# Segment attention in two layer pairs: a new layout for stored keys and queries, one kept set of output weights, a split last value projection, and regrouped closing norms

## The chip, the cores and the metric

The kernel runs on one core of a Trainium2 chip. A core has several engines, each with its own queue of instructions that it works through in order: TensorE (PE in the profile) multiplies matrices and writes to PSUM, VectorE (DVE) and ScalarE (ACT) work element by element and move PSUM results to SBUF, GpSimd (POOL) does small copies here, and SyncE (SP) issues transfers. SP, ACT and POOL each issue DMA transfers, which 16 DMA engines carry out; main memory is called DRAM. Engines wait for each other by semaphores.

The metric is the time of one execution on the device in microseconds (us). The time before is the median of three runs.

## What is computed

Four residual layers follow each other, A, B, A, B, here numbered 0 to 3. The input is 2048 rows of 640 numbers.

```python
def _A_ref(x, mem0, Wq, Wk, Wv, Wo, seg_len):        # 32 heads of 192, seg_len 32, 8 memory rows
    mem = mem0
    for s in range(n_seg):                             # 64 segments, one after the other
        h = jnp.concatenate([mem, x[:, 32*s:32*s + 32, :]], axis=1)      # 40 rows
        q, k, v = (einsum('btd,dhe->bhte', h, W) for W in (Wq, Wk, Wv))
        p = softmax(where(mask, einsum('bhqe,bhke->bhqk', q, k) * scale, -1e9))
        o = einsum('bhte,hed->btd', einsum('bhqk,bhke->bhqe', p, v), Wo)
        mem = o[:, :M, :]                              # the next segment's memory rows
        outs.append(o[:, M:, :])
    return jnp.concatenate(outs, axis=1)

def _B_ref(x, wqkv, w_phi, wo):                        # linear attention, 32 heads of 20
    ...
    o = num / den
    return o.reshape(B, S, D) @ wo

x = x + _A_ref(_layernorm(x), ...)
x = x + _B_ref(_layernorm(x), ...)
x = x + _A_ref(_layernorm(x), ...)
x = x + _B_ref(_layernorm(x), ...)
```

A segment's memory rows are an output of the segment before it, so the 64 segments of a layer A form a chain: 8 output rows have to be complete before the next segment's first projection can start.

## The kernel before

**Layer A** (`layer_A`, L632) has three parts.

*Preparation* (`A_pre`, L718). Of the 32 input rows of a segment the last 8, its tail rows, don't take part in what the chain hands on, apart from their keys and values being seen by others. Their queries, keys and values are computed ahead for all segments in large matmuls. The work is cut into two halves `h` of 32 segments and four rounds `r` of 8 heads. Each (half, round) computes K and Q for 256 rows into a staging tile `st` (two of them take turns, `sts`, in the space `wo_mid` that later holds output weights) and stores it to DRAM in one transfer, `kqb_d` (L877, named kqb<-arena in the profile: a staging row holds 32 segments x 192 numbers for one of 128 partitions). This store goes through SP's queue in layer 0 and through ACT's in layer 2. V goes through two small tiles in `wo_end` to `vb_d` (L899, vb<-arena, 8 transfers on POOL's queue for each half and round). After the last rounds the output weights are loaded over the staging space (`early_wo`, `late_wo`, L702 to L707), so these loads wait for the stores to land.

*The chain* (`A_chain`, L905; the segment loop starts at L1108). The order of instructions is written by hand (`manual_schedule`). A segment runs its four rounds in the order 0, 1, 2, 3 when it is even and 3, 2, 1, 0 when it is odd; the last, 63, is odd. In each round PE projects Q and K (`q_or_k`) and V (`project`) from `hT`, the 32 chain rows of the segment: 8 memory rows and 24 input rows. Each projection has five steps `b` of four matmuls. The weights of rounds 1 and 2 stay in SBUF, as do those of the steps 0 and 1 of rounds 0 and 3; the steps 2 to 4 of rounds 0 and 3 share slots, which SP refills during a segment's first round for its last (`load_slot`, L665 and L670). The prepared tail keys and queries are read back with `load_kqb` (L946, L948 at the DMA; one transfer per segment and round on POOL's queue, two rounds ahead into two buffers) and copied beside the chain's own by POOL (`extra_kq`, L951 to L956); tail values come by `extra_v` (L960, Vp<-vb). Then `scores` (L1014, L1019), an exponential on ACT (`weigh`, L1072), column sums on PE (`sums`, L1086), a reciprocal by Ln and Exp on ACT and a multiply on DVE (`normalise`, L1091 to L1093), and `attend` (L1027) follow. A round's attention runs while the next round's projections do. The results of the 32 chain rows are multiplied by the round's output weights into `W` (`wo_round`, L1049, matmul at L1054, 12 steps of four matmuls); those of the 8 tail rows are kept and stored (`keep_tail`, `store_tail`, L1047, otb<-otb). The output weights of rounds 1 and 2 stay in `wo_mid`; those of rounds 0 and 3 share `wo_end`, so that `load_wo` (L682, loads at L687 and L689) fetches the set of the segment's last round when the set of its first has been used. `keep_busy` adds matmuls without use.

*The closing product* for the tail rows (`post_steps`, L1224, matmuls at L1243 and L1244): in groups of 16 segments, the stored tail results are fetched (`fetch_tails`, L1210), rearranged (`spread_tails`), and multiplied by all four sets of output weights. For this the last segment loads both sets, 0 and 3, one into `wo_end`, one into `low`, the space of the resident projection weights.

**Layer B** (`layer_B`, L248) ends in a loop over four groups `g` of 512 rows: `attention` computes six column chunks `c`, each with two products (L559) and a spread of the denominators (L562) on PE, a copy on ACT (L564) and a multiply on DVE (L565); `output_rows` multiplies by `wo` (L410), adds the residual for four row blocks of 128 and stores them. In layer 1 the layer norm for the next layer A is worked out on the way: `ln_moments` (L217, DVE), `ln_deviation` (L229, ACT), `ln_apply` (L237, DVE and ACT), then a store to `xnext_dram`. `finish_rows` (L572) does the last two for a row block of the group before, called inside the attention. Layer 3 has no such norm.

The DMA semaphores of a queue are used in turn: before an issue, the engine waits until the transfer that used that semaphore last has landed.

Of the kernel before, what the change touches and what calls it, by code (L numbers as in the profile page):

```python
# [8 lines left out]
P = 128  # L9
BF16 = mybir.dt.bfloat16  # L10
F32 = mybir.dt.float32
ACT = mybir.ActivationFunctionType
ALU = mybir.AluOpType
# [102 lines left out]
class Kernel:  # L116
# [131 lines left out]
    def layer_B(self, x_dram, at_dram, xout_dram, xnext_dram, li, bp, post):  # L248


        nc, tc, KC, D = self.nc, self.tc, self.KC, self.Dm
# [14 lines left out]
        wo = self.view(take(NC_ * D * 2), NC_ * D * 2).rearrange("p (c m) -> p c m", m=D)  # L266
# [24 lines left out]
        with tc.tile_pool(name=f"B{li}_kv", bufs=1, space=bass.MemoryType.PSUM, reuse_waits="tile") as kvp, \  # L291
# [260 lines left out]
            def attention(g, hl):  # L552
                tk = slice(512 * g, 512 * g + 512)
                oT = oTs.next().rearrange("p (c t) -> p c t", c=NC_)
                for c in range(NC_):
                    mc = sizes[c]
                    pn = bank("ps_num")
                    for sg in range(2):
                        nc.tensor.matmul(pn[0:mc, :], lhsT=kvm[0:mc, sg, c, 0:mc], rhs=phi[0:mc, sg, c, tk], start=(sg == 0),  # L559
                                         stop=(sg == 1))  # L560
                    pe = bank("ps_e")
                    nc.tensor.matmul(pe[0:mc, :], lhsT=expc[0:64, c, 0:mc], rhs=hl, start=True, stop=True)  # L562
                    rx = rxs.next()
                    nc.scalar.activation(out=rx[0:mc, :], in_=pe[0:mc, :], func=ACT.Copy)  # L564
                    nc.vector.tensor_tensor(out=oT[0:mc, c, :], in0=pn[0:mc, :], in1=rx[0:mc, :], op=ALU.mult)  # L565
                    if c > 0:
                        finish_rows()
                return oT

            unfinished = []  # L570

            def finish_rows():  # L572
                if unfinished:
                    ob, m, rows = unfinished.pop(0)
                    xn = xns.next()
                    self.ln_apply(bp, ob, m, self.ln_deviation(bp, m), xn, True)
                    nc.gpsimd.dma_start(out=xnext_dram[rows, :], in_=xn[:])

            def output_rows(g, oT):
                for b in range(4 * g, 4 * g + 4):  # L580
# [7 lines left out]
                    if xnext_dram is not None:  # L588
                        unfinished.append((ob, self.ln_moments(bp, ob, 6), rows))

            hl = [denominators(0, side_bank), denominators(1, bank)]
            for g in range(NG):
# [5 lines left out]
                output_rows(g, oT)  # L598
            while unfinished:
                finish_rows()  # L600
# [31 lines left out]
    def layer_A(self, xn_dram, at_dram, li, x_raw=None):  # L632
# [4 lines left out]
        PW = 1536  # L637
        self.kqb_d = dram.tile([NSEG, P, NR, 192], BF16, name=f"kqb{li}")
        self.vb_d = dram.tile([NSEG, NR, 2, 8, 896], BF16, name=f"vb{li}")
# [78 lines left out]
    def A_pre(self, xn_dram, li, load_matrix, piece, wo_mid, wo_end, lay_out_wo, early_wo, x_raw):  # L718
# [12 lines left out]
        with ExitStack() as es:  # L731
# [102 lines left out]
            for h, ri, r in steps:  # L834
# [41 lines left out]
                stq = nc.scalar if x_raw is None else nc.sync  # L876
                stq.dma_start(out=self.kqb_d[SH * h:SH * h + SH, :, r, :].rearrange("s p f -> p s f"), in_=st)  # L877
                if x_raw is not None:
# [26 lines left out]
    def A_chain(self, xn_dram, at_dram, li, load_slot, piece, load_wo, late_wo, wo_mid, wo_end, low):  # L905
# [3 lines left out]
        with tc.tile_pool(name=f"A{li}_ch", reuse_waits="tile", bufs=1) as sp, \  # L909
# [36 lines left out]
            def load_kqb(s, r):  # L946
                kqb = sp.tile([P, 192], BF16, name="kqb", tag="kqb", bufs=2)
                nc.gpsimd.dma_start(out=kqb[:], in_=self.kqb_d[s, :, r, :])  # L948
                return kqb
# [96 lines left out]
            def store_tail(otb, s, r):  # L1046
                nc.gpsimd.dma_start(out=self.otb_d[:, s, 96 * r:96 * r + 96], in_=otb[:, :, :].rearrange("p c t -> p (c t)"))  # L1047

            def wo_round(W, r, OT, first, last, part=range(12)):  # L1049
                w = wo_end[:, :] if r in (0, 3) else wo_mid[:, 7680 * (r - 1):7680 * r]  # L1050
                for i in part:
# [56 lines left out]
            for s in range(NSEG):  # L1108
                W = pop.tile([P, 512], F32, name="ps_w", tag="w")
                order = rounds(s)  # L1110
                L = NR - 1

                def q_or_k(m, n):
# [23 lines left out]
                v_rows(pv, 0)  # L1137
                Ep = None
                for n in range(L):
                    raw = q_or_k("Q", n + 1)  # L1140
# [13 lines left out]
                    if n == 1:  # L1154
                        wo_round(W, order[n - 1], OT, True, False)
                        if n == 1:
                            load_wo(order[L])
                            if s == NSEG - 1:
                                tails = [self.fetch_tails(0, low)]
                                load_wo(3, low[:, 0:7680])  # L1160
                                tails.append(self.fetch_tails(1, low))
                    if n + 1 < L:
# [4 lines left out]
                pv = v_banks()  # L1167
                project(hT, pv, "V", L, s, range(KC))
                v_rows(pv, L)
                OT1 = OT  # L1170
                wo_round(W, order[L - 2], OT1, False, False, range(4))
                S, E = weigh(True)
# [4 lines left out]
                store_tail(otb, s, order[L - 1])  # L1177
                wo_round(W, order[L - 2], OT1, False, False, range(4, 6))
                sums(S, E)
                wo_round(W, order[L - 2], OT1, False, False, range(6, 12))  # L1180
                normalise(S, E)
# [42 lines left out]
    def post_steps(self, ops):  # L1224

        nc = self.nc
        at_dram, wo_mid, wo_end, low = self.post_args
        wo = [wo_end[:, :], wo_mid[:, 0:7680], wo_mid[:, 7680:15360], low[:, 0:7680]]

# [58 lines left out]
```

## Time and profile before

| | |
|---|---|
| runs | 3598.71, 3606.52, 3606.56 us, median 3606.52 |
| profiled execution | 3619.27 us; span 3617.5 us; mean granted TensorE clock 0.992 |
| bytes moved by DMA | 933.32 MB in 517,905 packets, 141,066 of them under 512 B |
| L977, projections, ps_qk and ps_v on PE | 998.2 + 519.2 us busy |
| L1054, output weights on PE | 18,432 matmuls, 451.7 us busy |
| layer 0, chain of segments | from 168.4 us to about 1546 us |
| layer 2, chain of segments | from 1980.9 us to about 3364 us |

A row of the profile names line, engine, operation and tiles (written <- read), partitions x elements, and how often (x). In a timeline the first two numbers are the start and the duration in us, and the brackets hold the engine's idle time before and what ended it. In the list of DMA issues come the KB of one transfer and the median time from issue to landing. The queues q1 and q10 are those that SP and ACT issue to, q0 is POOL's. The granted clock is the share of TensorE's full clock that its throttle let through; where it is below 1, matmuls take longer.

### The profile page before, as it was taken

The page shows a single profiled execution, that of the slowest core. Times are in us where ns is not written, and L with a number is a line of the kernel's source. Part 1 is how long each engine was busy: PE and PEld are TensorE (multiplying, and loading weights), DVE is VectorE, ACT ScalarE, POOL GpSimd, SP SyncE. Part 2 cuts the span into 40 slices and gives each one's busy share as a digit, 9 for nine tenths or more (in the row PEclk, how much of TensorE's full clock was granted, in tenths as well). Part 3 has the DMA queues.
Part 4 walks back from the last instruction along what each step waited for, and adds up shares of the span by engine and source line. Part 5 has one row for each costly group of instructions (what it writes and reads, how often), then busy time and mean ns, then how long its engine had stood idle before and what let it go on. Part 6 is the DMA issues. An engine that isn't in the chain of part 4 may idle for free.

```text
span 3617.5 us, 168478 instructions
## 1 busy us (share of the span) xinstructions
PE 3470.1 (96%) x70978; PEld 2278.5 (63%) x71399; DVE 2329.5 (64%) x6320; ACT 2030.9 (56%) x5233; POOL 1592.2 (44%) x4173
## 2 busy tenths in 40 slices
PE   9989999999999999999999899999999999999999
PEld 7756666666666666655377566666666666666553
DVE  5556666666666666646633566666766666666465
ACT  3346666666666656646423566666666566656463
POOL 3445555555545545530123455555555555554400
PEclk9999999999999999999999999999999999999999
DMA  9988888888888878860487888887888888878700
GB/s 302 331 294 281 289 286 282 289 289 289 278 284 291 288 269 285 293 235 1 148 271 215 289 276 287 290 283 271 292 291 280 274 289 291 287 270 278 248 1 30
DMA packets 517905, 933.32 MB, mean 258 GB/s; under 512 B 141066, under 2 KB 284058, under 8 KB 516122
## 3 DMA queue, kind: packets, MB, share of 16 engines
q1 hardware_dynamic: 415738, 821.50, 64.7%
q0 software_dynamic: 67744, 87.80, 8.3%
q10 hardware_dynamic: 33664, 13.24, 1.5%
q8 instruction: 557, 9.13, 1.0%
q14 instruction: 202, 1.65, 0.1%
HBM read 852.43 MB, written 73.73 MB: 256 GB/s over the span
## 4 chain that ended last, share of the span: by engine, by line
PE 59%; DMA 23%; DVE 6%; ACT 6%; issue 4%; POOL 2%; SPq 0%; POOLq 0%; ACTq 0%; DVEq 0%
PE ps_qk L977 17%; DMA arena<-wo_rows 12%; PE ps_w L1054 6%; PE ps_v L977 5%; DMA arena<-in_A_Wv_dram 5%; PE ps_pre L867 5%; PE ps_o L1027 3%; PE ps_s L1019 3%; PE ps_pre L891 2%; PE ps_s L1086 2%; PE kv L1243 2%; DVE E L1093 2%; DMA Vp<-vb 2%; ACT raw L987 2%; DVE hT L932 2%
## 5 line engine op out<-in xcount | busy, mean ns | idle before, releaser
L977 PEld LDWEIGHTS <-hT 128*32 128x32 bf16 x30720 | 757.1, 96 | 457.3 <-issue 34.8
L977 PE MATMUL ps_qk<-arena,hT 128*32 128x384 bf16 x20480 | 998.2, 327 | 10.0 <-DMA arena<-in_A_Wk_dram 2.0
L987 ACT ACTIVATE raw<-ps_qk 128x384 bf16<-128x384 f32 x1024 | 503.1, 491 | 378.4 <-PE ps_s L1086 249.3
L977 PE MATMUL ps_v<-arena,hT 128*32 128x384 bf16 x10240 | 519.2, 329 | 19.6 <-DMA arena<-in_A_Wv_dram 18.9
L960 POOL DMA_DIRECT2D Vp<-vb x512 | 258.3, 505 | 625.0 <-PE ps_o L1027 477.5
L1054 PE MATMUL ps_w<-arena,OT 128*32 128x160 bf16 x18432 | 451.7, 235 | 26.1 <-DMA arena<-wo_rows 25.3
L992 DVE STREAM_TRANSPOSE KT<-raw 128x384 bf16<-128x384 bf16 x512 | 296.0, 578 | 194.3 <-ACT raw L987 190.3
L1054 PEld LDWEIGHTS <-OT 128*32 128x32 bf16 x18432 | 324.7, 96 | 118.5 <-issue 40.8
L995 DVE STREAM_TRANSPOSE QT<-raw 128x256 bf16<-128x256 bf16 x512 | 227.9, 445 | 238.6 <-ACT raw L987 196.0
L948 POOL DMA_DIRECT2D kqb<-kqb x512 | 291.9, 570 | 174.5 <-POOL KT L956 146.7
L1008 DVE CAST Vp<-ps_v 64x384 bf16<-64x384 f32 x512 | 285.9, 558 | 113.5 <-ACT Vp L1006 101.8
L1093 DVE TENSOR_TENSOR E<-E,ps_s 80x320 bf16<-80x320 bf16 x512 | 247.3, 483 | 151.6 <-ACT ps_s L1092 150.5
L1047 POOL DMA_DIRECT2D otb<-otb x512 | 283.1, 553 | 139.6 <-DVE otb L1043 106.0
L1006 ACT ACTIVATE Vp<-ps_v 64x384 bf16<-64x384 f32 x512 | 245.2, 479 | 134.9 <-PE ps_v L977 134.4
L1072 ACT ACTIVATE E<-ps_s 80x320 bf16<-80x320 f32 x512 | 221.8, 433 | 87.1 <-PE ps_s L1019 47.7
L1027 PEld LDWEIGHTS <-Vp 80*128 80x128 bf16 x4096 | 188.9, 98 | 120.6 <-issue 95.3
L1027 PE MATMUL ps_o<-E,Vp 80*128 80x80 bf16 x4096 | 232.7, 201 | 29.0 <-DMA Vp<-vb 7.5
L940 ACT ACTIVATE Vp<-ps_w 32x160 bf16<-32x160 f32 x512 | 150.7, 294 | 158.4 <-DVE wt L1203 146.0
L953 POOL COPY QT<-kqb 128x64 bf16<-128x64 bf16 x512 | 125.7, 246 | 253.5 <-PE ps_s L1019 245.7
L1091 ACT ACTIVATE ps_s<-ps_s 80x320 f32<-80x320 f32 x512 | 214.9, 420 | 36.6 <-PE ps_s L1086 36.6
L1019 PE MATMUL ps_s<-QT,KT 128*80 128x80 bf16 (+1 forms) x3072 | 233.2, 213 | 1.8 <-POOL KT L956 1.7
L1033 ACT ACTIVATE OT<-ps_o 128x192 bf16<-128x192 f32 x384 | 125.4, 327 | 169.3 <-PE ps_o L1027 169.3
(156 smaller groups left out, 5516.7 us busy)
## 6 DMA issues: line engine op xcount, KB each, us to landing
arena<-wo_rows SPq DMA_DIRECT2D x792, 320.0 KB, 7.0
arena<-in_A_Wq_dram SPq DMA_DIRECT2D x427, 384.0 KB, 4.9
arena<-in_A_Wv_dram SPq DMA_DIRECT2D x427, 384.0 KB, 6.3
arena<-in_A_Wk_dram SPq DMA_DIRECT2D x768, 192.0 KB, 5.0
kqb<-kqb POOLq DMA_DIRECT2D x512, 48.0 KB, 5.1
arena<-in_A_Wk_dram SPq DMA_DIRECT2D x43, 384.0 KB, 6.6
vb<-arena POOLq DMA_DIRECT2D x128, 112.0 KB, 6.1
Vp<-vb POOLq DMA_DIRECT2D x512, 28.0 KB, 4.7
```

The costliest lines, as they stand in the source:

```text
L948: nc.gpsimd.dma_start(out=kqb[:], in_=self.kqb_d[s, :, r, :])
L960: nc.gpsimd.dma_start(out=Vs[n % 2][64:80, :], in_=self.vb_d[s, r].rearrange("g t f -> (g t) f"))
L977: nc.tensor.matmul(o[32 * g:32 * g + 32, 0:384], lhsT=hT[:, b, :], rhs=rhs, start=(i == 0), stop=(i == KC - 1), tile_position=(0, 32 * g), ...
L987: nc.scalar.activation(out=raw[:], in_=ps[:, 0:384], func=ACT.Copy)
L992: nc.vector.transpose(out=KT[:, :, 0:64], in_=raw[:, :].rearrange("p (c j) -> p c j", j=64))
L1006: nc.scalar.activation(out=o, in_=i, func=ACT.Copy)
L1008: nc.vector.tensor_copy(out=o, in_=i)
L1019: nc.tensor.matmul(S[0:80, c0:c0 + 80 * (q1 - q0)], lhsT=KT[:, 3 * x + i, :], rhs=QT[:, x, q0:q1, :], start=False, stop=(x == 1 and i == 2 ...
L1027: nc.tensor.matmul(O[x][:, 80 * i:80 * i + 80], lhsT=Vs[n % 2][0:80, 448 * x + k:448 * x + k + 128], rhs=E[0:80, 160 * x + 80 * e:160 * x ...
L1047: nc.gpsimd.dma_start(out=self.otb_d[:, s, 96 * r:96 * r + 96], in_=otb[:, :, :].rearrange("p c t -> p (c t)"))
L1054: nc.tensor.matmul(W[32 * g:32 * g + 32, 0:160], lhsT=OT[:, c, q:q + 32], rhs=w[:, 640 * i + 160 * g:640 * i + 160 * g + 160], start=(firs ...
L1093: nc.vector.tensor_tensor(out=E[0:80, 0:320], in0=E[0:80, 0:320], in1=rc, op=ALU.mult)
```

## The change

Four parts, of which the first three are in layer A.

1. `kqb_d` is laid out with the round first, then the partition, then the segment. The store of a half and round then writes, for each partition, 32 segments in one piece; the load of one segment and round reads 128 pieces of 192 numbers, as before, from rows that lie 64 x 192 numbers apart instead of 4 x 192.
2. In the last segment, the output weights of its last round (round 0) are loaded into `low` right after the first V projection, and stay there for the closing product; `wo_end` keeps round 3. The load of round 3 into `low` is gone, and both tail fetches follow each other.
3. In a segment's last round the V projection is cut after two of its five steps, and six steps of output weights stand in between. Before, four stood after the whole projection. The later pieces change from 4 to 6 and 6 to 12 into 6 to 8 and 8 to 12.
4. In layer B's output stage two of a group's four row blocks are measured (`ln_moments`) at once, as before, and the other two in the next group's attention, at chunks 0 and 2. `finish_rows` is called at chunks 2 to 5 instead of 1 to 5, and both are put in the queues behind that chunk's copy and multiply (`issue_after`). The closing loop runs over the four last row blocks.

```diff
@@ -561,17 +561,25 @@
                     pe = bank("ps_e")
                     nc.tensor.matmul(pe[0:mc, :], lhsT=expc[0:64, c, 0:mc], rhs=hl, start=True, stop=True)
                     rx = rxs.next()
-                    nc.scalar.activation(out=rx[0:mc, :], in_=pe[0:mc, :], func=ACT.Copy)
-                    nc.vector.tensor_tensor(out=oT[0:mc, c, :], in0=pn[0:mc, :], in1=rx[0:mc, :], op=ALU.mult)
-                    if c > 0:
-                        finish_rows()
+                    spread = nc.scalar.activation(out=rx[0:mc, :], in_=pe[0:mc, :], func=ACT.Copy)
+                    scaled = nc.vector.tensor_tensor(out=oT[0:mc, c, :], in0=pn[0:mc, :], in1=rx[0:mc, :], op=ALU.mult)
+                    with tc.issue_after(spread.ins), tc.issue_after(scaled.ins):
+                        if c in (0, 2):
+                            measure_rows()
+                        if c > 1:
+                            finish_rows()
                 return oT
 
-            unfinished = []
+            written, measured = [], []
+
+            def measure_rows():
+                if written:
+                    ob, rows = written.pop(0)
+                    measured.append((ob, self.ln_moments(bp, ob, 6), rows))
 
             def finish_rows():
-                if unfinished:
-                    ob, m, rows = unfinished.pop(0)
+                if measured:
+                    ob, m, rows = measured.pop(0)
                     xn = xns.next()
                     self.ln_apply(bp, ob, m, self.ln_deviation(bp, m), xn, True)
                     nc.gpsimd.dma_start(out=xnext_dram[rows, :], in_=xn[:])
@@ -586,7 +594,9 @@
                         nc.vector.tensor_tensor(out=ob[:, lo:hi], in0=ps[:, 0:hi - lo], in1=x2[:, b, lo:hi], op=ALU.add)
                     (nc.sync if xnext_dram is None else nc.gpsimd).dma_start(out=xout_dram[rows, :], in_=ob[:])
                     if xnext_dram is not None:
-                        unfinished.append((ob, self.ln_moments(bp, ob, 6), rows))
+                        written.append((ob, rows))
+                        if b < 4 * g + 2:
+                            measure_rows()
 
             hl = [denominators(0, side_bank), denominators(1, bank)]
             for g in range(NG):
@@ -596,7 +606,8 @@
                 elif g + 1 < NG:
                     hl.append(denominators(g + 1, side_bank))
                 output_rows(g, oT)
-            while unfinished:
+            for _ in range(4):
+                measure_rows()
                 finish_rows()
 
     def build_A_consts(self):
@@ -635,7 +646,7 @@
         dram = self.dram
         NR = 4
         PW = 1536
-        self.kqb_d = dram.tile([NSEG, P, NR, 192], BF16, name=f"kqb{li}")
+        self.kqb_d = dram.tile([NR, P, NSEG, 192], BF16, name=f"kqb{li}")
         self.vb_d = dram.tile([NSEG, NR, 2, 8, 896], BF16, name=f"vb{li}")
         self.otb_d = dram.tile([P, NSEG, 384], BF16, name=f"otb{li}")
         wview = self.wview
@@ -874,7 +885,7 @@
                 if x_raw is None and h == NH - 1 and ri == NR - 1:
                     early_wo()
                 stq = nc.scalar if x_raw is None else nc.sync
-                stq.dma_start(out=self.kqb_d[SH * h:SH * h + SH, :, r, :].rearrange("s p f -> p s f"), in_=st)
+                stq.dma_start(out=self.kqb_d[r, :, SH * h:SH * h + SH, :], in_=st)
                 if x_raw is not None:
                     if h == 0 and ri + 1 < NR:
                         for m in "KQV":
@@ -945,7 +956,7 @@
 
             def load_kqb(s, r):
                 kqb = sp.tile([P, 192], BF16, name="kqb", tag="kqb", bufs=2)
-                nc.gpsimd.dma_start(out=kqb[:], in_=self.kqb_d[s, :, r, :])
+                nc.gpsimd.dma_start(out=kqb[:], in_=self.kqb_d[r, :, s, :])
                 return kqb
 
             def extra_kq(kqb):
@@ -1046,8 +1057,10 @@
             def store_tail(otb, s, r):
                 nc.gpsimd.dma_start(out=self.otb_d[:, s, 96 * r:96 * r + 96], in_=otb[:, :, :].rearrange("p c t -> p (c t)"))
 
+            last_wo = None
+
             def wo_round(W, r, OT, first, last, part=range(12)):
-                w = wo_end[:, :] if r in (0, 3) else wo_mid[:, 7680 * (r - 1):7680 * r]
+                w = low[:, 0:7680] if last_wo == r else wo_end[:, :] if r in (0, 3) else wo_mid[:, 7680 * (r - 1):7680 * r]
                 for i in part:
                     c, q = i % 6, 32 * (i // 6)
                     for g in range(4):
@@ -1109,6 +1122,8 @@
                 W = pop.tile([P, 512], F32, name="ps_w", tag="w")
                 order = rounds(s)
                 L = NR - 1
+                if s == NSEG - 1:
+                    last_wo = order[L]
 
                 def q_or_k(m, n):
                     ps = pqp.tile([P, 512], F32, name="ps_qk", tag="qk")
@@ -1136,6 +1151,8 @@
                 project(hT, pv, "V", 0, s, range(KC))
                 v_rows(pv, 0)
                 Ep = None
+                if s == NSEG - 1:
+                    load_wo(order[L], low[:, 0:7680])
                 for n in range(L):
                     raw = q_or_k("Q", n + 1)
                     if n > 0:
@@ -1154,30 +1171,30 @@
                     if n == 1:
                         wo_round(W, order[n - 1], OT, True, False)
                         if n == 1:
-                            load_wo(order[L])
-                            if s == NSEG - 1:
-                                tails = [self.fetch_tails(0, low)]
-                                load_wo(3, low[:, 0:7680])
-                                tails.append(self.fetch_tails(1, low))
+                            if s < NSEG - 1:
+                                load_wo(order[L])
+                            else:
+                                tails = [self.fetch_tails(tb, low) for tb in range(2)]
                     if n + 1 < L:
                         pv = v_banks()
                         project(hT, pv, "V", n + 1, s, range(KC))
                         v_rows(pv, n + 1)
                     Ep = E
                 pv = v_banks()
-                project(hT, pv, "V", L, s, range(KC))
+                OT1 = OT
+                project(hT, pv, "V", L, s, range(2))
+                wo_round(W, order[L - 2], OT1, False, False, range(6))
+                project(hT, pv, "V", L, s, range(2, KC))
                 v_rows(pv, L)
-                OT1 = OT
-                wo_round(W, order[L - 2], OT1, False, False, range(4))
                 S, E = weigh(True)
                 OT, o = attend(Ep, L - 1, KT[:, :, 0:64])
                 tails_after(L - 1)
                 otb = keep_tail(o, True)
                 next_kq(s, L)
                 store_tail(otb, s, order[L - 1])
-                wo_round(W, order[L - 2], OT1, False, False, range(4, 6))
+                wo_round(W, order[L - 2], OT1, False, False, range(6, 8))
                 sums(S, E)
-                wo_round(W, order[L - 2], OT1, False, False, range(6, 12))
+                wo_round(W, order[L - 2], OT1, False, False, range(8, 12))
                 normalise(S, E)
                 if s + 1 < NSEG:
                     hT = new_hT()
@@ -1225,7 +1242,7 @@
 
         nc = self.nc
         at_dram, wo_mid, wo_end, low = self.post_args
-        wo = [wo_end[:, :], wo_mid[:, 0:7680], wo_mid[:, 7680:15360], low[:, 0:7680]]
+        wo = [low[:, 0:7680], wo_mid[:, 0:7680], wo_mid[:, 7680:15360], wo_end[:, :]]
 
         def fetch(tb):
             return self.fetch_tails(tb, low)
```

## The prediction

> **What bounds the kernel now.** I read the page's busy totals and the chain that ended last, then the windows of each layer's start, PE's list of waits, and the timelines there.
>
> ```profile
> PE 3470.1 (96%) x70978; PEld 2278.5 (63%) x71399; DVE 2329.5 (64%) x6320; ACT 2030.9 (56%) x5233; POOL 1592.2 (44%) x4173
> ...
> PE 59%; DMA 23%; DVE 6%; ACT 6%; issue 4%; POOL 2%; SPq 0%; POOLq 0%; ACTq 0%; DVEq 0%
> ```
>
> PE is busy for 3470.1 of 3617.5 us, so an edit that moves no arithmetic can win little beyond 147 us, and DMA is the next on the chain. The 147 us are not even:
>
> ```profile
> 168.40:208.30 39.90, 26.66 (x515) 0.79 0.89 293
> 208.30:229.30 21.00, 20.62 (x514) 1.00 0.81 283
> 1980.90:2018.00 37.10, 26.91 (x515) 0.77 0.85 283
> ```
>
> Columns: stretch, length, PE busy and instructions, granted clock, DMA share, GB/s. The rows are the first and second segment of layer 0 and the first of layer 2. A settled segment lasts 21 us; the first ones take 18.9 and 16.1 us more, with a clock of 0.79 and 0.77.
>
> **Part A, kqb by round and row.** Bytes and issue counts stay. Each of 16 stores changes from 4096 runs of 384 B to 128 rows of 32 x 384 = 12,288 B.
>
> ```profile
> q1 hardware_dynamic: 415738, 821.50, 64.7%
> ...
> q10 hardware_dynamic: 33664, 13.24, 1.5%
> ...
> kqb<-kqb POOLq DMA_DIRECT2D x512, 48.0 KB, 5.1
> ...
> kqb<-arena SPq DMA_DIRECT2D x8, 1536.0 KB, 15.6
> otb<-otb POOLq DMA_DIRECT2D x512, 24.0 KB, 4.8
> ...
> kqb<-arena ACTq DMA_DIRECT2D x8, 1536.0 KB, 8.3
> ```
>
> q10 is nearly all kqb stores of layer 2 (8 x 4096 = 32,768 of 33,664 packets): 1.5% of 16 x 3617.5 us is 868 us, 25.8 ns a packet, 15.3 GB/s per engine. q1 carries weights: 64.7% gives 90 ns a packet of 1976 B, 21.9 GB/s. The Trainium skill ("DMA: Bandwidth & Descriptors", Specifications) puts line rate at 512 B and up; by that alone a store (98 KB per engine) goes from 6.4 to 4.5 us, 2 us won. But the rows show 15.6 us, not 6.4: each small packet waits for others. With one q1 packet after each of its 256 packets per engine a store needs 256 x (25.8 + 90 ns) = 29.6 us; the measured 15.6 lies between. If the rows travel in packets like q1's, with turns shared equally, a store needs 2 x 4.5 = 9 us. I take 9 (6 to 15.6, the last if nothing merges).
>
> What a store holds up in layer 0 is SP and the last vb stores:
>
> ```profile
> 162.63 0.77 SPq L877 DMA_DIRECT2D kqb<-arena  x1
> ...
> 178.39 0.89 SPq L689 DMA_DIRECT2D arena<-in_A_Wo_dram  x2
> 179.65 1.38 SPq L687 DMA_DIRECT2D arena<-wo_rows  x3
> ```
> ```profile
> 185.27 0.46 PE L1054 MATMUL ps_w<-arena,OT 128*32 128x160 bf16 x8 [6.17 <-DMA arena<-wo_rows]
> ...
> 197.99 0.51 PE L977 MATMUL ps_v<-arena,hT 128*32 128x384 bf16 x4 [3.63 <-DMA arena<-in_A_Wv_dram]
> ```
>
> The store issued at 162.63 lands at 178.4; until then SP can't load into its staging (L689). The three loads at 179.65 wait for the last vb stores, which landed at 179.63 because POOL stood 1.97 us at 174.19 behind a kqb load that took 6.0 us. With the store down at about 172, two 320 KB loads leave the stretch (640 KB at its some 320 GB/s, 2.0 us), and that load should take 3.3 us (as the one issued at 176.53 did), which brings the vb landings and the loads behind them 2.6 us forward. From 179.65 to 200 DMA is full (share 0.99 to 1.06), so Wv comes 4.6 us sooner. PE's waits there (6.17, 0.35, 0.34, 0.39, 3.63, 0.88, 0.26 = 12.0) fall by 4.6. **Clock**: busy time times clock lost is 4.04 x 0.50 + 3.97 x 0.12 + 1.03 x 0.20 + 4.84 x 0.49 = 5.1 us in 185 to 205. The Trainium skill ("TensorE: Matmul & The Clock Gate", Part 1) halves the clock after an idle window of about 3.4 us; the first wait would be cut to some 3, so by the rule all 5.1 would come back. The trace speaks against it: a 2.89 us wait at 1884.04 was followed by 0.57. I count half, 2.4. Sum **-7** (-3 to -11).
>
> Layer 2, preparation: stores on ACT's queue take up to 22.3 us beside weight loads, and the staging tile is wanted before that:
>
> ```profile
> 1883.29 1.29 DVE L87 CAST arena<-ps_pre 128x512 bf16<-128x512 f32 x2 [6.73 <-DMA kqb<-arena]
> ```
>
> PE then waits 2.89, and 1884 to 1888 runs at 0.57 (4.0 x 0.43 = 1.7). A store 6.7 us quicker ends both: **-4.5** (-2 to -5). SP's wait of 14.6 at L676 goes too, but loads were ahead of PE there. Layer 2's first segment (10 us of PE waits) hangs on vb landings, and its last store took only 7.8: **-2** (-6 to +2).
>
> The 512 loads keep 128 runs of 384 B; their row pitch goes from 1,536 to 24,576 B. The nearest row has 192 B runs at 49,152 B pitch (otb<-otb, 4.8 us). Against 5.1 now: **0** (-2, +100, see the rivals).
>
> **Part B, one set of output weights.** Each layer A drops 6 of 12 closing loads (1.9 MB, 6.6 us at 289 GB/s). The other 6 follow the last segment's slot loads on SP (the last at 1532.79) where they were issued at 1534.51, and both tail fetches come next. PE stood 3.83 us before the closing product (1550.02), behind an eviction that waited 4.99 for the first fetch. That fetch (1538.97) was ahead of the dropped loads (1539.35), and the DMA share is 1.02 to 1.05 from 1530 to 1545, so the same bytes still go before it: it gains the 1.2 us at most. The second fetch lands some 6 us sooner, but PE waits at that eviction only once a layer. The moved loads need nothing that is still in use but can crowd the V slots: two layers, **-1** (-4 to +3).
>
> **Part C, V split in the last round.** PE's instruction count is unchanged; 24 output matmuls (about 0.5 us) enter the V projection, 16 leave its end. This has two sides:
>
> ```profile
> 244.34 0.48 DVE L1093 TENSOR_TENSOR E<-E,ps_s 80x320 bf16<-80x320 bf16 x1 [0.18 <-ACT ps_s L1092]
> ...
> 246.75 0.48 DVE L1093 TENSOR_TENSOR E<-E,ps_s 80x320 bf16<-80x320 bf16 x1 [0.72 <-ACT ps_s L1092]
> ```
> ```profile
> 244.35 0.45 PE L1019 MATMUL ps_s<-QT,KT 128*80 128x80 bf16 x6
> 244.88 0.45 PE L1027 MATMUL ps_o<-E,Vp 80*128 80x80 bf16 x8
> ...
> 247.53 0.46 PE L1027 MATMUL ps_o<-E,Vp 80*128 80x80 bf16 x8
> ```
>
> The product at 244.88 starts 0.06 us after the multiply at 244.34 ends (244.82): it waited. PE's list has only 3.0 us of such waits, as short ones are left out; start by start the third product of a segment waits 0.23 us in over half of 128 segments, 22 us in all. Eight more matmuls ahead (0.17 us) take most of it. But the fourth product (247.53) loses those eight between its sum at 245.51 and itself; it is 0.30 after its multiply here, 0.13 in the median, so some segments pay there. With both limits, segment by segment, an estimate of -7. The split also gives the Wv slots 0.5 us more: their waits are 3.7 us (8 times) in layer 0 and 6.3 (13) in layer 2 behind the start, but DMA is 0.8 to 0.9 full and the output-weight waits (5.6 and 9.9) may take them over; I count nothing. Vp's copies come 0.5 us later, still a microsecond ahead of their product. **-6** (-12 to +5).
>
> **Part D, closing norms (first layer B only).** PE waits for copies that stand behind norms on ACT:
>
> ```profile
> 1789.56 10.20 PE L410 MATMUL ps_wo<-arena 120*128 120x512 bf16 x48 [2.20 <-ACT arena L564]
> ```
>
> Such waits are 5.6 us there, and the clock is 0.81 in 1787 to 1805. Against the other layer B, which has no norms, the stage takes 9.6 us more, the most to be won. A norm is 1.4 us of ACT; 3 instead of 4 now stand before the last copy, but two row measurements (1.24 us each on DVE) come into the attention: DVE then has 6 multiplies of 0.69, 2.5 of statistics and 4 x 0.31, 7.9 us, against ACT's 3.6 + 4.2 = 7.8 where it had 9.2. So 1.3 us for each of three groups at most: **-3** (-8 to +2).
>
> **Sum.** -7 - 4.5 - 2 + 0 - 1 - 6 - 3 = -23.5. The profiled execution took 3619.3 (span 3617.5 and 1.8 around it), so it would take about 3596. The median of the runs shown is 3606.5, 12.8 below it; the same difference gives **3583 us**.
>
> **Rivals.** (1) The store is quicker, but the starts stay bound by vb landings and a full DMA, and C gives back at the fourth product what it wins at the third: A 4.5, D 2 remain, 3600. For it: DMA share near 1 at the starts. Against: 0.56 from 175 to 180, when SP stood. (2) **Slower**: the loads at 24 KB pitch. POOL's copies wait for PE (245.7 us, 125 times) and for a kqb load only 6 times (6.9 us); the slack between landing and copy is 1.2 us in the worst twentieth and below 2.1 in a quarter. So nothing happens up to +1.2 us; at +3, 128 loads would be late by about 1 us each, and scores (L1019) follow the copies directly: +100, 3683; at +2 about +30, 3613. For it: the stride is 16-fold. Against: the otb row. (3) The stores gain nothing (the rows go on as 384 B packets): B, C and D remain, -10, 3597. For it: source and destination are both described in 384 B pieces in the loop over segments, which nothing in the trace shows merged. (4) V's split costs 0.17 us at the fourth product in every segment and wins nothing: +21 against A and D, 3608.
>
> **Chances.** About 0.3% (10.8 us) tells a run of this kernel from no change. Forecast 0.56; (1) 0.14, (2) 0.12, (3) 0.12, (4) 0.06. Faster takes the forecast, (3) where C is full, and a part of (1): 0.70; same 0.16; slower 0.14. The likeliest case's own bounds are 3562 to 3598; the range reaches up to 3606 for (1) and (3).
>
> **What would show it.** kqb<-arena near 9 us on both queues and far fewer packets of 384 B (141,066 under 512 B, less some 65,000); kqb<-kqb within 0.5 us of 5.1; first segments some 7 and 2 us shorter at a higher clock; no wait near 1884; the third product's start 0.04 us after the scores; L687 six loads fewer per layer. I'm wrong if kqb<-kqb takes 7 us or more, if the waits for E at the fourth product pass 20 us, or if the first segments keep their 39.9 and 37.1 us.

## The result, and the profile after

| | before | after |
|---|---|---|
| median of 20 runs each | 3606.4 us (3598.7 to 3614.9) | 3598.2 us (3585.7 to 3609.6) |
| ratio of the runs, 95% interval | | 0.9976 (0.9966 to 0.9985) |
| profiled execution | 3619.3 us | 3592.2 us |

The change makes the kernel 0.24% faster, 8.7 us (5.4 to 12.3). The forecast was 23.5. The two profiled executions differ by 27 us: the one of before lies above all 20 runs of its kernel, the one of after 6 us below its median. Two single profiles can't show where 8.7 us went, so the readings below are held against those of all the experiments.

The transfers did what the forecast said. These are lines of the queue table (packets, MB, share of 16 engines) and of the list of DMA issues of the changed kernel (issues: KB of one, median us to landing):

```profile
q1 hardware_dynamic: 382266, 817.56, 64.0%
...
q10 hardware_dynamic: 1920, 13.24, 0.9%
...
kqb<-kqb POOLq DMA_DIRECT2D x512, 48.0 KB, 5.1
...
kqb<-arena SPq DMA_DIRECT2D x8, 1536.0 KB, 6.6
...
kqb<-arena ACTq DMA_DIRECT2D x8, 1536.0 KB, 7.2
```

ACT's queue q10 sent 33,664 packets before and sends 1920 now: 31,744 fewer, which is 8 stores x (4096 - 128), so a row of 12,288 B went as one packet. SP's stores land in 6.6 us instead of 15.6, better than the 9 that were taken. The loads at the wider pitch take 5.1 us as before.

The same windows as before (stretch, length, PE busy and instructions, clock, DMA share, GB/s), for the first and second segment of layer 0 and the first of layer 2:

```profile
170.45:205.58 35.13, 26.43 (x515) 0.81 0.82 285
205.58:226.58 21.00, 20.31 (x509) 1.00 0.81 283
1969.00:2004.65 35.65, 26.02 (x515) 0.81 0.81 279
```

The first segment of layer 0 is 4.8 us shorter, but it starts 2.1 us later, and the clock hardly rises (0.79 to 0.81). The timelines of SP and PE there show what still waits:

```profile
164.68 0.34 SPq L888 DMA_DIRECT2D kqb<-arena  x1
...
172.76 7.20 SPq L698 DMA_DIRECT2D arena<-wo_rows  x3
180.05 1.33 SPq L681 DMA_DIRECT2D arena<-in_A_Wq_dram  x3
```
```profile
181.80 0.32 PE L1067 MATMUL ps_w<-arena,OT 128*32 128x160 bf16 x8 [0.37 <-DMA arena<-wo_rows]
...
185.66 0.35 PE L988 MATMUL ps_qk<-arena,hT 128*32 128x384 bf16 x4 [0.68 <-DMA arena<-in_A_Wq_dram]
...
196.09 0.51 PE L988 MATMUL ps_v<-arena,hT 128*32 128x384 bf16 x4 [2.50 <-DMA arena<-in_A_Wv_dram]
```

The store lands at 170.4 (before 178.4), and SP goes on at once. But its next loads over the V staging still wait until 178.85 (before 179.65) for the last vb stores. PE's waits for output weights, 6.17 us before, are below 1 us each; waits for Wq come in, and that for Wv is 2.50 (3.63 before).

### The profile page after: what moved, and what is told of

Its sections match the earlier page's. It is cut to its first block, busy times and chain, and to the rows that moved or that the text cites. A ratio compares the mean times of both kernels' runs of the same rounds, so it can differ in the third digit from the quotient of the medians.

```text
span 3590.5 us, 168460 instructions
## 1 busy us (share of the span) xinstructions
PE 3465.5 (97%) x70978; PEld 2268.6 (63%) x71399; DVE 2327.0 (65%) x6320; ACT 2032.0 (57%) x5233; POOL 1589.1 (44%) x4173
## 3 DMA queue, kind: packets, MB, share of 16 engines
q10 hardware_dynamic: 1920, 13.24, 0.9%
## 4 chain that ended last, share of the span: by engine, by line
PE 55%; DMA 20%; issue 9%; DVE 7%; POOL 5%; ACT 4%; SPq 1%; PEld 0%; POOLq 0%; ACTq 0%; DVEq 0%
PE ps_qk L988 17%; DMA arena<-wo_rows 7%; DMA Vp<-vb 6%; PE ps_v L988 6%; PE ps_w L1067 6%; PE ps_pre L878 3%; PE ps_o L1038 3%; PE ps_s L1030 3%; DVE hT L943 2%; PE ps_s L1099 2%; DMA arena<-in_A_Wv_dram 2%; PE ps_s L1025 2%; PE ps_pre L902 2%; PE ps_idle L1074 2%; PE kv L1260 1%
## 5 line engine op out<-in xcount | busy, mean ns | idle before, releaser
L988 PEld LDWEIGHTS <-hT 128*32 128x32 bf16 x30720 | 746.5, 96 | 431.9 <-DVE hT L1221 27.2
L988 PE MATMUL ps_v<-arena,hT 128*32 128x384 bf16 x10240 | 534.6, 328 | 8.7 <-DMA arena<-in_A_Wv_dram 8.4
L1067 PE MATMUL ps_w<-arena,OT 128*32 128x160 bf16 x18432 | 446.1, 234 | 11.4 <-DMA arena<-wo_rows 10.4
L1030 PEld LDWEIGHTS <-KT 128*80 128x80 bf16 x3072 | 205.4, 119 | 28.7 <-issue 18.3
```

What stands on the lines that cost most here:

```text
L988: nc.tensor.matmul(o[32 * g:32 * g + 32, 0:384], lhsT=hT[:, b, :], rhs=rhs, start=(i == 0), stop=(i == KC - 1), tile_position=(0, 32 * g), ...
L1030: nc.tensor.matmul(S[0:80, c0:c0 + 80 * (q1 - q0)], lhsT=KT[:, 3 * x + i, :], rhs=QT[:, x, q0:q1, :], start=False, stop=(x == 1 and i == 2 ...
L1067: nc.tensor.matmul(W[32 * g:32 * g + 32, 0:160], lhsT=OT[:, c, q:q + 32], rhs=w[:, 640 * i + 160 * g:640 * i + 160 * g + 160], start=(firs ...
```

## The experiments

Times are ratios to the kernel before, run on the same chips, with 95% intervals; us are that ratio times the median of before.

**The four parts alone.** Each kernel is the one before with one part of the diff.

Layout alone:

> Only the new layout of the stored keys and queries. Theory 1 (the layout carries the gain of the whole change, the split of V gives nothing): 6 to 10 us faster than before, stores near 6.5 us on both queues, first segment of layer 0 near 35 us, no wait near 1884, settled segments as before. Theory 2 (the starts stay bound by the vb landings and a full DMA, and the gain is the split's): 0 to 3 us faster.

Output weights alone:

> Only the kept set of output weights in the last segment. Both theories: 0 to 3 us faster, within what can be told from no change; 12 loads at L687 fewer; the closing product starts 0.5 to 1.5 us sooner in each layer A.

Split of V alone:

> Only the split of the last round's V projection. Theory 1: within 3 us of before, because what the third product of a segment wins the fourth product and the last pieces of output weights give back. Theory 2: 5 to 10 us faster, settled segments shorter by 0.05 us or more on the mean.

Norms alone:

> Only the regrouped closing norms. Both theories: 1 to 4 us faster; the wait of the output product for ACT's copy in layer 1 down from 2.0 to 2.2 us in each group to about 1, the stretch from layer 1's output stage to the next preparation 2 us shorter.

All but the split:

> The changed kernel without the split of V: layout, output weights and norms. If the split only shifts a wait: 5 to 8 us below before, within 3 us of the changed kernel. If the split gives what was forecast for it (6 us): 2 us below before.

| kernel | ratio | us |
|---|---|---|
| layout | 0.9989 (0.9977 to 1.0001) | -4.0 |
| output weights | 0.9997 (0.9983 to 1.0012) | -1.1 |
| split of V | 0.9994 (0.9980 to 1.0008) | -2.2 |
| norms | 0.9995 (0.9981 to 1.0009) | -1.8 |
| layout, output weights and norms | 0.9983 (0.9970 to 0.9996) | -6.1 |

No part alone is clear of noise, but their sum, -9.1, is close to the whole change's -8.7. The split is worth -2.2 alone and -2.6 as the difference between the whole and the last row, which lies where "only shifts a wait" put it. Theory 1 (the layout carries nearly all) expected 6 to 10 for the layout, theory 2 5 to 10 for the split: both miss, though the intervals reach into both ranges. What the layout's interval does exclude is the 13.5 us that the prediction gave it.

**Why the split gives little.** PE's list of waits has one for the tail values (us in total, times, longest), first before, then after:

```profile
PE ps_o L1027 <- DMA Vp<-vb: 7.5, 17, 1.2
```
```profile
PE ps_w L1067 <- issue: 16.4, 36, 1.2
PE ps_o L1038 <- DMA Vp<-vb: 15.0, 39, 1.0
```

In five other kernels without the split it is 9.3 to 13.5, so only a part of the doubling is the split's. The fourth product of a segment needs the tail values of the last round. POOL loads them when the second product has freed their buffer. In the segment that the prediction showed, POOL's timeline has that load:

```profile
241.73 0.51 POOL L960 DMA_DIRECT2D Vp<-vb  x1 [1.68 <-PE ps_o L1027]
```

The trace has its landing at 247.49, and the fourth product started at 247.53, 0.22 us later than the matmuls ahead of it would have let it. Load by load, the fourth product starts less than 0.3 us after the landing in 81 of 128 segments before and in 99 after. The next runs take this wait away.

```diff
 def extra_v(s, n):
     r = rounds(s)[n]
-    nc.gpsimd.dma_start(out=Vs[n % 2][64:80, :], in_=self.vb_d[s, r]...)
+    p0 = 80 if n == NR - 1 else 64
+    nc.gpsimd.dma_start(out=Vs[n % 2][p0:p0 + 16, :], in_=self.vb_d[s, r]...)
```

Loads to spare rows:

> The kernel before, with the tail values of each segment's last round loaded into rows that no product reads (same bytes, same issue; the last round's product takes the values of an earlier round, so the output is not the reference's). Theory 3 (the fourth product of a segment is bound by the landing of these values, which start only when the second product has freed their buffer): 4 to 12 us faster than before; the fourth product starts 0.04 us after the matmul ahead of it in more than half of the segments. Rival (it is bound by the multiply E, or by nothing): within 2 us of before.

With the split:

> The split of V together with the same loads into rows that no product reads (output as in the run with these loads alone). Theory 3: the split now pays: 4 to 12 us faster than the run with the loads alone, because its gain at the third product is no longer taken back at the fourth. Rival (the split gives nothing because the multiply E is late at the fourth product): within 2 us of the run with the loads alone, the fourth product starting 0.05 us after its multiply in most segments.

With the whole change:

> The changed kernel with the tail values of each segment's last round loaded into rows that no product reads (output not the reference's, as in the runs with these loads before). If the landing of these values is what holds the changed kernel's segments too: 12 to 18 us below the changed kernel, 20 to 26 below before. If the gain of these loads and the gains of the change are the same microseconds: 16 below before.

| kernel | ratio | us | second to fourth product, median us |
|---|---|---|---|
| before | 1 | | 6.73 |
| split alone | 0.9994 | -2.2 | 6.69 |
| spare rows | 0.9954 (0.9938 to 0.9970) | -16.6 | 6.35 |
| spare rows and split | 0.9949 (0.9934 to 0.9964) | -18.4 | 6.37 |
| spare rows and whole change | 0.9940 (0.9918 to 0.9961) | -21.6 | 6.50 |

With nothing waiting for these bytes, PE's list in the kernel with spare rows has

```profile
PE ps_o L1028 <- DVE E L1094: 4.0, 6, 1.3
PE ps_o L1028 <- DMA Vp<-vb: 1.0, 1, 1.0
```

and 16.6 us are won, twice what the whole change brought and more than the 4 to 12 expected. On the changed kernel the same loads win 12.9 us, so the two gains are for the most part different microseconds. The first half of theory 3 stands: this landing holds the segment. One rival is in the edit itself: a load to spare rows doesn't wait for the second product (in this segment of the kernel with spare rows it goes out at 237.15, with no wait before it), so POOL goes on to its next copies, those for the scores ahead of the third product, without the 1.68 us. But the time from the second to the third product is 3.90 us in the median with and without spare rows, and that from the third to the fourth falls from 2.72 to 2.43, so the gain lies where the landing was.

The second half of theory 3 is not borne out: the split gives 1.8 us here, too little to tell from nothing, and the rival expected up to 2. With spare rows and split the third product's start falls from 0.27 to 0.13 us after the matmul ahead of it, as the forecast said; the fourth's rises from 0.04 to 0.09 in the median, and in half of the segments it now starts 0.05 us after its multiply ends. The eight matmuls that cover the third product are missing at the fourth. Summed over 128 segments, the waits are:

| | third product | fourth product |
|---|---|---|
| usual loads, no split (mean of six kernels) | 27 us | 22 us |
| usual loads, split (mean of two) | 11 | 32 |
| spare rows, no split | 26 | 4 |
| spare rows and split | 13 | 10 |

So the fourth product takes back 10 of 16 us with the usual loads, most of it by the landing, and 6 of 13 with spare rows, by the multiply. More goes at a third place. Between the two products PE stands ahead of the sixth of 48 output-weight matmuls, and the profile names nothing that ends this wait ("issue", the first line after above). With the split this wait is longer in each pair: 16.4 us in the changed kernel against 9.4 in the same without the split, 22.9 against 17.2 with spare rows (the profile of before has 17.4, too). What PE waits for there stays open. The time from second to fourth product changes by 0.04 us at most with the split, in both pairs.

**A reorder to start that load sooner.** The second product goes between the steps of the Q projection that it followed; the load that it releases moves with it (shown in short, for `n == 2`).

```diff
-raw = q_or_k("Q", n + 1)                 # at n == 2
-OT, o = attend(Ep, n - 1)
+project(hT, ps, "Q", n + 1, s, range(2))
+OT, o = attend(Ep, n - 1)
+project(hT, ps, "Q", n + 1, s, range(2, KC))
+raw = to_raw(ps, "raw")
```

On the kernel before:

> The kernel before, with the second product of a segment moved between the second and third of the five steps of the Q projection that it followed (reorder only, nothing left out). If the landing of the last round's tail values sets the fourth product, their load starts 0.5 us sooner and 8 to 16 us of the 16 that the run without these loads won come back with the right output. If that run won for another reason (for example because less waits for the DMA queue), 0 to 3 us.

On the changed kernel, with the rows of the next experiment:

> The changed kernel with the second product moved likewise and with the norms' input rows loaded one block further ahead. If the parts add: 8 to 16 us below the changed kernel (3598), 16 to 24 below before.

On the changed kernel without the split of V:

> As the changed kernel, but without the split of V and with the second product moved: layout, output weights, norms and the moved product. If the split only shifts a wait from the third to the fourth product, this is within 3 us of the run that has the split; if the split pays once the tail values are early, it is 4 to 8 us slower.

Measured: 1.0011 (1.0000 to 1.0023), 0.9979 (0.9965 to 0.9994) and 0.9991 (0.9976 to 1.0005). The wait did go: on the kernel before the landing now comes 0.7 us ahead of the fourth product in the median, and only 15 of 128 start less than 0.3 us after it. Yet nothing is won, and the parts don't add. (The last two differ by 4.3 us in favour of the split, with the norms' rows in it: between the two expectations, and too close to the noise to decide.) PE's timeline of the first of these kernels shows the price:

```profile
241.95 0.50 PE L977 MATMUL ps_qk<-arena,hT 128*32 128x384 bf16 x8
242.38 0.46 PE L1027 MATMUL ps_o<-E,Vp 80*128 80x80 bf16 x8
242.78 0.67 PE L977 MATMUL ps_qk<-arena,hT 128*32 128x384 bf16 x12
243.38 0.33 PE L1014 MATMUL ps_s<-mask_st,ident 80*80 80x320 bf16 x1
```

From the projection to the scores it takes 1.42 us in nearly every segment; in the order of before (240.06 to 241.27 in the segment shown) 1.21 for the same 28 matmuls. Going from projection matmuls on 32 columns to a product on 128 columns and back once more costs 0.21 us, 27 us over 128 segments. That is enough to use up what the earlier load wins. The second expectation of this run, that the 16.6 us came from a lighter queue, has nothing for it: the bytes were the same.

**Why the layout gives less in layer 0.** The kernel with the layout alone reaches the first segment at 169.6, 1.3 us late. Its DVE timeline in the preparation (idle time and releaser in brackets):

```profile
117.97 0.89 DVE L222 BATCH_NORM_STATS2 ln_stats<-ln_x 128x6 f32<-128x320 bf16 x2 [5.87 <-DMA ln_x<-in_A_x_dram]
...
137.84 0.43 DVE L918 MEMSET Vp<- 128x448 uint32 x1 [5.62 <-DMA xn<-ln_xn]
138.19 3.01 DVE L87 CAST arena<-ps_pre 128x512 bf16<-128x512 f32 x5
...
146.82 0.72 DVE L932 STREAM_TRANSPOSE hT<-Vp 32x160 bf16<-32x160 bf16 x2 [5.62 <-DMA Vp<-xn]
```

In the kernel before, the same two later waits are shorter:

```profile
132.59 0.43 DVE L918 MEMSET Vp<- 128x448 uint32 x1 [3.23 <-DMA xn<-ln_xn]
...
140.45 0.71 DVE L932 STREAM_TRANSPOSE hT<-Vp 32x160 bf16<-32x160 bf16 x2 [0.65 <-DMA Vp<-xn]
```

DVE works in order. While it stands for small loads of POOL's queue, evictions (copies of PSUM results to SBUF) pile up (five in a row at 138.19). Before, the issue of SP's next load behind the slow store at 106 took 10.9 us, and in that time POOL's rows came quicker: the load issued at 107.56 took 5.9 us. With the quick store SP streams weights from 107.7 on, and the same load takes 9.1. The test loads the rows one block further ahead:

```diff
-v["x"] = lp.tile([P, self.Dm], BF16, name="ln_x")
+v["x"] = lp.tile([P, self.Dm], BF16, name="ln_x", bufs=3)
 ...
-out = [lists[0][0]]
+out = [t[0] for t in lists[:2]]
 for i, t in enumerate(lists):
-    if i + 1 < len(lists):
-        out.append(lists[i + 1][0])
+    if i + 2 < len(lists):
+        out.append(lists[i + 2][0])
     out += t[1:]
```

> The new layout, with the input rows of the norms in layer 0's preparation loaded one row block further ahead (three buffers instead of two). Theory 4 (the quicker stores let SP's weight loads run ahead, these make POOL's small loads late, DVE waits for them and its evictions come late): the first segment starts at 168.4 to 169.2 instead of 169.6 (layout alone), the waits of DVE for ln_x go. Rival (the later start is chance): unchanged at 169.6 or anywhere from 168 to 171 without relation to DVE's waits. The time is 0 to 2 us below the layout alone.

Measured: first segment at 168.25, time 0.9991 (0.9975 to 1.0007). In its DVE timeline no wait for ln_x is left after 41 us, and the two later waits are

```profile
133.44 0.43 DVE L918 MEMSET Vp<- 128x448 uint32 x1 [4.19 <-DMA kqb<-arena]
...
141.00 0.71 DVE L932 STREAM_TRANSPOSE hT<-Vp 32x160 bf16<-32x160 bf16 x2 [1.32 <-DMA Vp<-xn]
```

Start times of whole profiles also move in the first 20 us, by up to 1.4 us against before and with no relation to the edits. Counted from matmul 900 to matmul 1250 of the preparation instead, the five kernels with the layout and the old loads come 0.7 to 2.8 us (mean 1.2) later than before, the two with the rows ahead 0.0, and six of the seven without the layout 0.0 to 0.1 (the other waited for Wq). Theory 4 fits all of this; its worth, about 1 us, is below what the times can tell.

No version with the complete computation beat the changed kernel: the best, with moved product and rows ahead, is level with it.

## The prediction, point by point

The sign was right and the first effect of each part is in the traces, but the sum was 2.7 times too large. **The failed step is the size of the two largest terms: of the 14.8 us that are missing, 9.5 are the layout's (forecast 13.5, measured 4.0) and 3.8 the split's (6 and 2.2).** In the layout's sum, the last vb landings came 1.8 us forward where 2.6 was taken, the clock gave nothing where 2.4 was taken, and layer 2's wait was taken from its longest case; the split's sum left out the landing of the tail values at the fourth product. The split's four pairs of kernels give 1.8 to 4.3 us, 2.7 on the mean, each within some 5 us. Stage by stage over all 14 profiles, seven with the layout and seven without (six and eight for the output weights and the norms):

| step | forecast | measured |
|---|---|---|
| layout, layer 0 start | -7 | first segment 36.6 against 39.3 us: -2.7; preparation +1.2 |
| layout, layer 2 preparation | -4.5 | 160.1 against 161.5 us: -1.4 |
| layout, layer 2 first segment | -2 | 36.8 against 37.1 us: -0.3 |
| layout, all (timed alone) | -13.5 | -4.0 |
| output weights | -1 | -1.1 timed; segment 63 to closing product -0.5 and -0.9 |
| split of V | -6 | -2.2 timed |
| norms | -3 | -1.8 timed; stage 60.1 against 63.6 us: -3.5 |

**Layer 0.** PE's waits there "fall by 4.6": PE's waits for DMA in the first segment are 11.4 us in the mean of the seven kernels without the layout (9.1 to 13.1) and 8.5 with it (7.5 to 9.3), so 2.9. "which brings the vb landings and the loads behind them 2.6 us forward": counted from the segment's start, the last one landed at 10.3 us without the layout (8.3 to 11.6, with the profile of before at 11.3) and at 8.5 with it, so 1.8 forward; between the two profiles it was 0.9 in absolute time (179.63 to 178.71), as the preparation ended 2.1 later in that of after, of which the layout's part is 0.7. These stores were issued 3.9 us sooner, but the loads that the quick store let go (170.55 to 172.76) ran beside the last four, which took 4.7 to 5.7 us where the four ahead of them took 2.8. The room that the slow store left to POOL's queue was not counted. "I count half" of the clock's 5.1 us: the mean granted clock of the segment is 0.80 without the layout and 0.79 with it, so nothing came back. The changed kernel runs at 0.50 from 188.8 to 202.5; in the 3.4 us before that PE was busy for 1.73, and its waits were 0.68, 0.64 and 0.77. The rule of 3.4 us of idle time that the prediction cites would have kept the full clock; the trace speaks against it more than the prediction allowed.

**Layer 2.** The wait at 1884 was real, and no kernel with the layout has it. But 2.9 us was the longest of seven: the others have 2.4, 2.0, 1.6, 1.3, 1.0 and none. The mean is 1.6, and the stage's -1.4 fits this. I took one event of one execution for the rule.

**Loads at the wide pitch** cost nothing, as the otb row said.

**Split.** The 0.23 us at the third product was there and fell to about 0.1. The failed step is the sentence on the fourth product: "it is 0.30 after its multiply here, 0.13 in the median". The median in that trace is 0.35, and such a distance says that the multiply is not what holds it. I modelled the multiply alone; the landing of the tail values was in the same trace, 0.04 us ahead of the product. The step listed the Wv slots, the output weights and V's copies as what could take the gain over, and neither this load nor PE's wait in the output weights. Rival (4), which wins nothing and costs 21 (by its own terms 3611, not 3608), is wrong too: the gain is about 2.

**Norms.** From PE's timeline in layer 1, first before, then after:

```profile
1807.64 7.41 PE L410 MATMUL ps_wo<-arena 120*128 120x512 bf16 x48 [1.40 <-ACT arena L564]
...
1817.81 13.27 PE L867 MATMUL ps_pre<-next_xT,arena 128*128 128x256 bf16 x120 [2.07 <-DVE ln_shift L242]
```
```profile
1779.50 9.03 PE L410 MATMUL ps_wo<-arena 120*128 120x512 bf16 x48 [0.68 <-ACT arena L564]
...
1795.60 7.76 PE L410 MATMUL ps_wo<-arena 120*128 120x512 bf16 x48 [0.17 <-DVE arena L565]
...
1807.78 2.53 PE L878 MATMUL ps_pre<-next_xT,arena 128*128 128x256 bf16 x11 [3.74 <-DVE ln_shift L242]
```

The waits of 2.20 and 1.40 fall to 0.68 and 0.17, the latter now for DVE, as worked out; PE's waits for ACT's copies there fall from 5.6 to 2.8 in all. The next preparation waits 3.74 where it waited 2.07, a cost that the sum had not. The forecast's size holds within the noise.

**Range and rivals.** 3598 lies inside the range, near its upper end, where rivals (1) and (3) were put. What happened is mostly (1): the stores are quicker, the starts stay bound by vb landings and a full DMA, and the split gives back most of its gain by the fourth product. It had 0.14. The slower rivals did not happen.

What stays open is the settled segments' length from profile to profile. Without the first segments, the two chains take 2639.9 us together in the profile of before, 2625 to 2629 in the other four without the layout and with the usual tail loads, and 2619 to 2622 in the six with it. This looks like 7 us for the layout, but with the spare rows it is 2608 and 2605 without and 2609 with it, and the profiled executions with the layout lie 1.5 to 11.0 us below their kernels' medians, which nothing here explains. The times hold for the layout: -4.0, with -8.3 to +0.4 around it.

## What to carry to other kernels

Compare the profiled execution with the spread of the runs before sizing waits from it; where it lies outside, its longest waits may be its own, and only those that return in every round can be summed. Before moving cover from one wait to another in an in-order engine, list all that the second one waits for, the start of each transfer included: a product that starts 0.04 us after a landing is likely held by it, even if the wait is too short for a list of waits. A slow transfer that blocks a queue also leaves room to others; ask what uses it.

## What was not expected of the hardware

A row of 12,288 B left as one packet, and 128 of these (1536 KB) landed in 6.6 us beside the weight stream, where 4096 of 384 B took 15.6. Putting a product on 128 columns between projection matmuls that use 32 columns cost 0.21 us per passage. The Trainium skill ("TensorEngine Tiling (Array Packing)", Key Properties) says that a change of tiling drains the engine, without a price; 0.21 us is what this case shows, though not that the drain is all of it. And the clock fell to 0.50 after 3.4 us in which PE was still busy half of the time and its longest wait was 0.77 us.
